# Attention with a mixture of experts: the ninth block's values in two column halves, its transposes behind the next pair's scores

## The chip, the cores and the metric

The kernel runs on one core of a Trainium2 chip. The metric is device time in microseconds, the median of several runs; lower is better. Engines are named as in the profile: PE (TensorE matmuls), PEld (its weight loads), DVE (VectorE), ACT (ScalarE), POOL (GpSimd), SP (SyncE, which issues most transfers here).

## What is computed

Attention over 8 batches of 8 heads with 576 tokens and 64 features a head. The first four heads see the last 32 tokens, the other four every fourth token of the last 128:

```python
scores = scale * np.matmul(q, k.transpose(0, 1, 3, 2))
mask_plain = (rel >= 0) & (rel < window)
mask_dil = (rel >= 0) & (rel < window * dilation) & (rel % dilation == 0)
...
attn = attn / (np.sum(attn, axis=-1, keepdims=True) + 1e-09)
return np.matmul(attn, v).astype(np.float32)
```

Its output, 4608 tokens of 512 features, goes to a layer of 8 experts (512 to 1024 to 512, with a maximum with zero between). Each token uses one expert: the one with the largest logit, or that of the token before it where a second gate says so. Everything is float32.

## The kernel before

**Stages.** The attention stage fills the first 153 us of the profiled span, and the experts' stage the rest. In the attention stage the work is cut by pair: two heads of one batch, 32 pairs in all. A pair's 576 tokens are nine blocks of 64 queries; each block looks at 96 keys, its own 64 and the 32 before them. The dilated heads' tokens are sorted by class beforehand, so that they too are a band.

**One pair.** `scores` multiplies keys by queries for nine blocks and two heads (L334), with a mask matmul ahead of the blocks that need no cut (L328); ACT takes the exponential (L341), DVE masks the other blocks (L339). The two heads lie on the two row halves of PE. `values` multiplies the exponentials by the values (L387); the value tile has a column of ones, so that column 64 of the result is the sum for the softmax. Two blocks lie beside each other on the two column halves of PE and so on the two partition halves of the output: slot k holds blocks 2k and 2k + 1. Nine blocks make five slots, and the fifth computes block 8 in both halves. Slots are taken in two groups, 0 and 1, then 2 to 4 (`HALVES`), each in a PSUM tile `pv`. For each group DVE takes the reciprocal of the sums into `rec` (L391) and multiplies (L392) into `x`, a tile that holds four heads (two pairs) of a batch.

**Two pairs.** After every second pair `turn` transposes `x` for the routing: eight full 128x128 transposes (L408), four for each pair, copied to `xt` by ACT (L409), and two of the last 64 tokens (L412), copied at once (L414). `store` writes `x` to memory in two transfers, the first 512 tokens (L422) and the last 64 (L424). There are 16 such turns.

**The order.** It is written out by hand for PE, DVE, POOL and SP; ACT's is left to the scheduler. The main loop runs over n from 0 to 33. In iteration n stand: the scores of pair n; POOL's copy of the 32 shared value rows of pair n + 1 (`share`, L279); a gap; the values of pair n - 1; in odd iterations from 3 on the turn of the two pairs before; a gap; the loads of pair n + 3 (`load_keys` L267, `load_values` L272); the store; and, late in the stage, one gather of routed rows on POOL (L855), with a small copy ahead of it that waits for `rec` (`paced`, L275). A gap takes steps of the routing from a list (`waiting`), each with a cost, as far as a credit allows. Among these are logits (L441), logits turned (L453), carries (L484, L494, L504), the choice (L510), places (L548, L549), products (L600), counts (L617), the table (L701) and the tokens of the early units (L718 on PE, L728 to L738 on DVE). After every fourth turn `route` puts a new group of such steps on the list.

**Buffers.** All PSUM tiles but the scores' come from one pool of four banks (`bank`), the scores from another of two. `x` has three buffers. `check` looks at all of `rec` at the end and decides whether an exact version has to run.

Of the kernel before, what the change touches and what calls it, by code (L numbers as in the profile page):

```python
# [10 lines left out]
F32 = mybir.dt.float32  # L11
# [4 lines left out]
Alu = mybir.AluOpType  # L16
# [6 lines left out]
P = 128  # L23
B, H, S, DH = 8, 8, 576, 64
D = H * DH
# [10 lines left out]

NP = H // 2
NPB = B * NP
SLOTS = (NB + 1) // 2
HALVES = ((0, 2), (2, SLOTS))  # L40
CB = 3
AHEAD = 4
WARM = 3
# [174 lines left out]
def whole(ctx, tc, exact, bad, qk, v, wgl, w1, w2, con, adm, msk, qmk, out, cst, wg, ones, warm):  # L218
# [32 lines left out]
    def bank(shape, name):  # L251
        return banks.tile(shape, F32, name=name, tag="bank")

    rec = once.tile([P, NPB, SLOTS, 2], F32, name="rec")
    pace = once.tile([1, 2], F32, name="pace")
    zero = work.tile([1, D // 2], F32, name="zero", bufs=1)
    nc.vector.memset(zero, 0.0)
# [14 lines left out]
        nc.sync.dma_start(out=vt[WIN:].rearrange("p u i e -> p (u i e)"), in_=v[n])  # L272

    def paced(n):
        nc.gpsimd.tensor_copy(pace, rec[:1, n, SLOTS - 1])  # L275

    def share(n):
        vt = vts[n % AHEAD]
# [36 lines left out]
    xs, prob, routes = {}, {}, {}  # L315

    def scores(n):

# [55 lines left out]
    def values(n):  # L374

        vt = loaded[n][2]
        if n % 2 == 0:
            xs[n // 2] = xp.tile([P, SLOTS, 2, 2, DH], F32, name="x")
        x = xs[n // 2]
        pr = prob.pop(n)  # L380
        for a, z in HALVES:
            pv = bank([P, z - a, 2, VW], "pv")
            for k in range(a, z):
                for u in range(2):
                    for h in range(2):
                        i = min(2 * k + h, NB - 1)
                        nc.tensor.matmul(pv[h * QB:(h + 1) * QB, k - a, u], lhsT=pr[i][:, u],  # L387
                                         rhs=vt[:, u, i], start=True, stop=True, tile_position=(0, h * QB),
                                         skip_group_check=True)
            r = rec[:, n, a:z]  # L390
            nc.vector.reciprocal(r, pv[:, :, :, DH])  # L391
            nc.vector.tensor_tensor(x[:, a:z, n % 2], pv[:, :, :, :DH],  # L392
                                    r.unsqueeze(3).to_broadcast([P, z - a, 2, DH]), op=Alu.mult)
        del loaded[n]

    def turn(m):

        x = xs[m]
        b, g = divmod(m, 2)
        if m % (2 * GB) == 0:  # L400
            routes[b // GB] = dict(xt=xtp.tile([P, 2, CH, GS], F32, name="xt"))
        xt = routes[b // GB]["xt"]
        s = b % GB * S
        full = S // P * P
        for c in range(CH):
            tp = bank([P, S // P, P], "tp")
            for k in range(S // P):
                nc.tensor.transpose(tp[:, k], x[:, k, c].rearrange("p u d -> p (u d)"), ident)  # L408
            nc.scalar.copy(xt[:, g, c, s:s + full], tp.rearrange("p k t -> p (k t)"))  # L409
        tp = bank([P, CH, S - full], "tp")  # L410
        for c in range(CH):
            nc.tensor.transpose(tp[:, c], x[:S - full, S // P, c].rearrange("p u d -> p (u d)"),  # L412
                                ident[:S - full, :S - full])
        nc.scalar.copy(xt[:, g, :, s + full:s + S], tp)  # L414

    def store(m):

        x = xs.pop(m)
        b, g = divmod(m, 2)
        full = S // P * P  # L420
        to = xd[g][b * S:(b + 1) * S]
        nc.sync.dma_start(out=to[:full].rearrange("(k p) f -> p k f", p=P),  # L422
                          in_=x[:, :S // P].rearrange("p k g u d -> p k (g u d)"))
        nc.sync.dma_start(out=to[full:], in_=x[:S - full, S // P].rearrange("p g u d -> p (g u d)"))  # L424

    def logits(g):

# [376 lines left out]
    def now(push):  # L804
        for f in push:
            f()
# [292 lines left out]
    for n in range(NPB + 2):  # L1099
        if n < NPB:  # L1100
            (scores_exact if exact else scores)(n)
        for k in range(NPB)[n + 1 if n else 0:n + 2]:
            share(k)
        gap(SHARE)
        if 1 <= n <= NPB:
            values(n - 1)
        if n == NPB + 1:
            assert len(rows) <= 4
            now(features(0))
        if n >= 3 and n % 2 == 1:  # L1110
# [30 lines left out]

    def check():

        flat = rec.rearrange("p n k u -> p (n k u)")
        fine = stage.tile([P, D], F32, name="y", bufs=3)[:, :NPB * SLOTS * 2]
# [8 lines left out]
        nc.vector.tensor_scalar(all_fine, lp, float(P * NPB * SLOTS * 2), None, Alu.is_lt)  # L1154
# [134 lines left out]
```

## Time and profile before

| What | us |
|---|---|
| median of 3 runs | 667.72 |
| lowest and highest run | 666.64, 669.94 |
| the profiled execution, own time | 663.76 |
| its span | 661.8 |
| PE busy in the span | 646.6 |
| DVE busy | 372.5 |
| ACT busy | 188.7 |
| POOL busy | 188.1 |

The span is the time from the first to the last instruction of the profiled execution; its own time holds 2.0 us around it. An instruction's busy time overlaps that of others on PE[...]. In the views below a group's line gives line, engine, operation, output<-inputs, shape and count, then busy us and mean ns of one, then the idle time of the engine ahead of it and what ended it.

### The profile page before, as it was taken

What the parts mean: (1) busy time and instruction counts of PE and PEld (TensorE: products, weight loads), DVE (VectorE), ACT (ScalarE), POOL (GpSimd) and SP (SyncE); (2) the same over time, 40 slices, a digit from 0 to 9 for tenths busy, and PEclk for the clock granted to TensorE, in tenths of its full rate; (3) what the DMA queues carried; (4) which work ended last, traced back from release to release, by engine and by line L of the source; (5) the groups of instructions that cost most, each with busy time, mean ns of one, the idle gap of its engine ahead of it and who ended that gap; (6) DMA issues with size and microseconds to landing.
All of it is one profiled execution on the core that took longest, in us unless ns stands there. A gap on an engine that the chain in (4) does not pass through costs nothing. (4 is left out here: it accounts for less than half of the span.)

```text
span 661.8 us, 15170 instructions
## 1 busy us (share of the span) xinstructions
PE 646.6 (98%) x6402; PEld 568.2 (86%) x6402; DVE 372.5 (56%) x755; ACT 188.7 (29%) x348; POOL 188.1 (28%) x169
## 2 busy tenths in 40 slices
PE   8999999999999999999999999999999999999996
PEld 6988888888588999999599989998899989899893
DVE  3558578683596595372537382727464536547441
ACT  3544343442112331222122222231222232223210
POOL 3322222242115420322552153223144113051011
PEclk9999999999999999999999999999999999999999
DMA  8999899749205398574533456541045451454001
GB/s 313 325 297 322 280 283 319 247 124 354 88 33 190 129 418 314 187 280 169 226 132 141 154 203 223 229 164 49 16 177 215 179 219 59 155 193 148 1 32 50
DMA packets 29356, 126.31 MB, mean 191 GB/s; under 512 B 4349, under 2 KB 13789, under 8 KB 25312
## 3 DMA queue, kind: packets, MB, share of 16 engines
q1 hardware_dynamic: 22480, 106.05, 44.4%
q0 software_dynamic: 6800, 19.21, 8.5%
q8 instruction: 52, 0.85, 0.5%
q14 instruction: 24, 0.20, 0.1%
HBM read 142.02 MB, written 19.20 MB: 244 GB/s over the span
## 5 line engine op out<-in xcount | busy, mean ns | idle before, releaser
L979 POOL DMA_INDIRECT out_dram<-y,tok x36 | 55.0, 1527 | 292.3 <-DVE y L1048 124.5
L951 PE MATMUL hp<-xc,sum 128*128 128x128 f32 x720 | 85.6, 275 | 0.4 <-DVE sum L818 0.4
L951 PEld LDWEIGHTS hp<-xc,sum 128*128 128x128 f32 x720 | 82.8, 192 | 0.8 <-PE hp L951 0.5
L1033 PE MATMUL yp<-sum,hc 128*128 128x256 f32 x360 | 82.6, 379 | 0.0
L961 DVE TENSOR_TENSOR h<-hp,h 128x512 f32<-128x512 f32 x45 | 30.9, 690 | 90.8 <-PE hp L951 90.1
L1033 PEld LDWEIGHTS yp<-sum,hc 128*128 128x128 f32 x360 | 68.3, 190 | 9.4
L1048 DVE SCALAR_TENSOR_TENSOR y<-yp,gate,y 128x256 f32<-128x256 f32 x45 | 21.7, 482 | 75.1 <-issue 48.1
L279 POOL COPY vt<-vt 32x1040 f32<-32x1040 f32 x32 | 34.0, 1065 | 94.2 <-DMA vt<-in_v_dram 63.0
L951 PE MATMUL hp<-xe,raw 128*128 128x128 f32 x480 | 58.8, 276 | 0.0
L951 PEld LDWEIGHTS hp<-xe,raw 128*128 128x128 f32 x480 | 56.6, 192 | 1.8 <-issue 1.5
L1033 PE MATMUL yp<-raw,h 128*128 128x256 f32 x240 | 57.0, 380 | 0.0
L334 PE MATMUL two<-kq 64*96 64x64 f32 x1152 | 54.5, 244 | 0.2 <-issue 0.2
L334 PEld LDWEIGHTS two<-kq 64*96 64x96 f32 x1152 | 53.7, 162 | 0.3 <-issue 0.3
L855 POOL DMA_INDIRECT xg<-xd,tok x40 | 45.5, 1138 | 27.3 <-PE hp L951 15.0
L1033 PEld LDWEIGHTS yp<-raw,h 128*128 128x128 f32 x240 | 44.4, 190 | 5.5
L955 ACT COPY h<-hp 128x512 f32<-128x512 f32 x45 | 26.4, 586 | 79.3 <-PE hp L951 75.3
L962 ACT ACTIVATE h<-h 128x512 f32<-128x512 f32 x45 | 28.3, 630 | 67.2 <-DVE h L961 67.2
L855 POOL DMA_INDIRECT xg<-xd,pos x40 | 44.1, 1102 | 11.8 <-issue 10.8
L339 DVE SCALAR_TENSOR_TENSOR pr<-two,mk 96x512 f32<-96x512 f32 x32 | 21.9, 685 | 43.8 <-ACT pr L341 32.3
L387 PE MATMUL pv<-vt,pr 96*64 96x65 f32 x1280 | 44.7, 224 | 1.0 <-POOL vt L279 1.0
L387 PEld LDWEIGHTS pv<-vt,pr 96*64 96x64 f32 x1280 | 40.2, 138 | 3.7 <-POOL vt L279 1.2
L1041 ACT ACTIVATE y<-yp,gate 128x256 f32<-128x256 f32 x45 | 21.2, 474 | 55.5 <-PE yp L1033 48.8
(223 smaller groups left out, 1004.6 us busy)
## 6 DMA issues: line engine op xcount, KB each, us to landing
raw<-in_w_dram SPq DMA_DIRECT2D x48, 2048.0 KB
kq<-in_qk_dram SPq DMA_DIRECT2D x32, 592.0 KB
vt<-in_v_dram SPq DMA_DIRECT2D x32, 292.5 KB
xd<-x SPq DMA_DIRECT2D x16, 512.0 KB
raw<-in_w_dram SPq DMA_DIRECT2D x4, 512.0 KB
xd<-x SPq DMA_DIRECT2D x16, 64.0 KB
xg<-xd,tok POOLq DMA_INDIRECT x40, 3.2
xg<-xd,pos POOLq DMA_INDIRECT x40, 3.4
```

The costliest lines, as they stand in the source:

```text
L279: nc.gpsimd.tensor_copy(vt[:WIN, :, 1:], vt[QB:, :, :NB - 1])
L334: nc.tensor.matmul(sc[:KW, u, k * QB:(k + 1) * QB], lhsT=kt[h, i * QB:i * QB + KW], rhs=qt[h, i * QB:(i + 1) * QB], start=bool(late), stop ...
L339: nc.vector.scalar_tensor_tensor(pr, sc[:KW, :, :w], -CEIL, mk[:, kind].unsqueeze(1).to_broadcast([KW, 2, w]), Alu.max, Alu.min)
L387: nc.tensor.matmul(pv[h * QB:(h + 1) * QB, k - a, u], lhsT=pr[i][:, u], rhs=vt[:, u, i], start=True, stop=True, tile_position=(0, h * QB), ...
L855: nc.gpsimd.indirect_dma_start(out=x[:rows, g], out_offset=None, in_=xd[g] if units[u]["late"] else xd[g][:EARLY * GS], in_offset=bass.Ind ...
L951: nc.tensor.matmul(to[:, m], lhsT=a[:, m, kk], rhs=b[:, kk], start=first and m == 0 and kk == 0, stop=(kk == DK // 2 - 1), skip_group_chec ...
L955: nc.scalar.copy(at((0, 1, 3)[k]), of)
L961: nc.vector.tensor_tensor(at(k), of, at(k), op=Alu.add)
L962: nc.scalar.activation(at(k), at(k), Act.Relu)
L979: nc.gpsimd.indirect_dma_start(out=out, out_offset=bass.IndirectOffsetOnAxis(ap=of_unit(u, "tok", j), axis=0), in_=y, in_offset=None, boun ...
L1033: nc.tensor.matmul(to, lhsT=a[:, m], rhs=b[:, m], start=first and m == 0, stop=(m == FK // 2 - 1), skip_group_check=True)
L1048: nc.vector.scalar_tensor_tensor(at(k), of, of_unit(u, "gate", k // 2), at(k), Alu.mult, Alu.add)
```

## The change

In `values` the fifth slot is no longer a slot of both heads and both halves. Block 8 of head u goes to column half u, so that two matmuls take the place of four, and one column of `pv` holds both heads. DVE takes 4 and 5 reciprocals instead of 4 and 6 (with one column of `rec` less), multiplies slots 2 and 3 as before, and multiplies the last column in an instruction of its own, which writes the result twice beside itself into a tile part `end`.

In `turn` the two transposes of the last 64 tokens become two full 128x128 transposes of `end`, each of a pair, and two ACT copies take a quarter of the result each (head u from partitions and columns of half u). They are not issued in `turn` but put on a list, which is run in the next iteration behind the scores and the gap, ahead of the values; in the four turns that a `route` follows, they are run at once. `store` writes the last 64 tokens in two transfers, one for each head of the pairs, in pieces of 64 floats.

```diff
-SLOTS = (NB + 1) // 2
-HALVES = ((0, 2), (2, SLOTS))
+FULLS = S // P
+HALVES = ((0, 2), (2, FULLS))
+SUMS = NB
...
-        nc.gpsimd.tensor_copy(pace, rec[:1, n, SLOTS - 1])
+        nc.gpsimd.tensor_copy(pace, rec[:1, n, SUMS - 2:])
...
+        def product(to, h, u, i):
+            nc.tensor.matmul(to[h * QB:(h + 1) * QB], lhsT=pr[i][:, u], rhs=vt[:, u, i], start=True, stop=True, tile_position=(0, h * QB), skip_group_check=True)
+
         for a, z in HALVES:
-            pv = bank([P, z - a, 2, VW], "pv")
+            last = z == FULLS
+            w = 2 * (z - a)
+            pv = bank([P, w + last, VW], "pv")
             for k in range(a, z):
                 for u in range(2):
                     for h in range(2):
-                        i = min(2 * k + h, NB - 1)
-                        nc.tensor.matmul(pv[h * QB:(h + 1) * QB, k - a, u], lhsT=pr[i][:, u],
-                                         rhs=vt[:, u, i], start=True, stop=True, tile_position=(0, h * QB),
-                                         skip_group_check=True)
-            r = rec[:, n, a:z]
-            nc.vector.reciprocal(r, pv[:, :, :, DH])
-            nc.vector.tensor_tensor(x[:, a:z, n % 2], pv[:, :, :, :DH],
-                                    r.unsqueeze(3).to_broadcast([P, z - a, 2, DH]), op=Alu.mult)
+                        product(pv[:, 2 * (k - a) + u], h, u, 2 * k + h)
+            if last:
+                for u in range(2):
+                    product(pv[:, w], u, u, NB - 1)
+            r = rec[:, n, 2 * a:2 * z + last]
+            nc.vector.reciprocal(r, pv[:, :, DH])
+            nc.vector.tensor_tensor(x[:, a:z, n % 2], pv[:, :w, :DH].rearrange("p (k u) d -> p k u d", u=2),
+                                    r[:, :w].rearrange("p (k u) -> p k u", u=2).unsqueeze(3).to_broadcast(
+                                        [P, z - a, 2, DH]), op=Alu.mult)
+            if last:
+                nc.vector.tensor_scalar(end[:, n % 2], pv[:, w:, :DH].to_broadcast([P, 2, DH]), r[:, w:], None, Alu.mult)
...
-        tp = bank([P, CH, S - full], "tp")
-        for c in range(CH):
-            nc.tensor.transpose(tp[:, c], x[:S - full, S // P, c].rearrange("p u d -> p (u d)"),
-                                ident[:S - full, :S - full])
-        nc.scalar.copy(xt[:, g, :, s + full:s + S], tp)
+
+        def ends():
+            tp = bank([P, CH, P], "tp")
+            for c in range(CH):
+                nc.tensor.transpose(tp[:, c], end[:, c].rearrange("p u d -> p (u d)"), ident)
+            for u in range(2):
+                h = slice(u * DH, (u + 1) * DH)
+                nc.scalar.copy(xt[h, g, :, s + full:s + S], tp[h, :, h])
+
+        behind.append(ends)
...
-        nc.sync.dma_start(out=to[full:], in_=x[:S - full, S // P].rearrange("p g u d -> p (g u d)"))
+        for u in range(2):
+            nc.sync.dma_start(out=to[full:].rearrange("t (g u d) -> t u g d", g=2, u=2)[:, u],
+                              in_=end[u * DH:(u + 1) * DH, :, 0])
...
         gap(SHARE)
+        now(behind)
+        behind.clear()
         if 1 <= n <= NPB:
             values(n - 1)
...
             if (n - 3) // 2 % (2 * GB) == 2 * GB - 1:
+                now(behind)
+                behind.clear()
                 route((n - 3) // 2 // (2 * GB), n == NPB + 1)
```

More of the change, by code (lines that the diff above doesn't have):

```diff
@@ L252, in bank @@
         return banks.tile(shape, F32, name=name, tag="bank")
-    rec = once.tile([P, NPB, SLOTS, 2], F32, name="rec")
+    rec = once.tile([P, NPB, SUMS], F32, name="rec")
     pace = once.tile([1, 2], F32, name="pace")
@@ L313, in load_first @@
                           in_=w1[i, :, part * rows * D:(part + 1) * rows * D])
-    xs, prob, routes = {}, {}, {}
+    xs, prob, routes, behind = {}, {}, {}, []
     def scores(n):
@@ L377, in values @@
         if n % 2 == 0:
-            xs[n // 2] = xp.tile([P, SLOTS, 2, 2, DH], F32, name="x")
-        x = xs[n // 2]
+            x = xp.tile([P, 4 * (FULLS + 1) * DH], F32, name="x")
+            xs[n // 2] = (x[:, :4 * FULLS * DH].rearrange("p (k g u d) -> p k g u d", k=FULLS, g=2, u=2),
+                          x[:, 4 * FULLS * DH:].rearrange("p (g u d) -> p g u d", g=2, u=2))
+        x, end = xs[n // 2]
         pr = prob.pop(n)
+        def product(to, h, u, i):
+            nc.tensor.matmul(to[h * QB:(h + 1) * QB], lhsT=pr[i][:, u], rhs=vt[:, u, i], start=True, stop=True, tile_position=(0, h * QB), skip_group_check=True)
         for a, z in HALVES:
-            pv = bank([P, z - a, 2, VW], "pv")
+            last = z == FULLS
+            w = 2 * (z - a)
+            pv = bank([P, w + last, VW], "pv")
             for k in range(a, z):
@@ L385, in values @@
                     for h in range(2):
-                        i = min(2 * k + h, NB - 1)
-                        nc.tensor.matmul(pv[h * QB:(h + 1) * QB, k - a, u], lhsT=pr[i][:, u],
-                                         rhs=vt[:, u, i], start=True, stop=True, tile_position=(0, h * QB),
-                                         skip_group_check=True)
-            r = rec[:, n, a:z]
-            nc.vector.reciprocal(r, pv[:, :, :, DH])
-            nc.vector.tensor_tensor(x[:, a:z, n % 2], pv[:, :, :, :DH],
-                                    r.unsqueeze(3).to_broadcast([P, z - a, 2, DH]), op=Alu.mult)
+                        product(pv[:, 2 * (k - a) + u], h, u, 2 * k + h)
[9 more added lines that the diff above has]
+                nc.vector.tensor_scalar(end[:, n % 2], pv[:, w:, :DH].to_broadcast([P, 2, DH]), r[:, w:], None, Alu.mult)
         del loaded[n]
     def turn(m):
-        x = xs[m]
+        x, end = xs[m]
         b, g = divmod(m, 2)
@@ L409, in turn @@
             nc.scalar.copy(xt[:, g, c, s:s + full], tp.rearrange("p k t -> p (k t)"))
-        tp = bank([P, CH, S - full], "tp")
-        for c in range(CH):
-            nc.tensor.transpose(tp[:, c], x[:S - full, S // P, c].rearrange("p u d -> p (u d)"),
-                                ident[:S - full, :S - full])
-        nc.scalar.copy(xt[:, g, :, s + full:s + S], tp)
+        def ends():
[6 more added lines that the diff above has]
+        behind.append(ends)
     def store(m):
-        x = xs.pop(m)
+        x, end = xs.pop(m)
         b, g = divmod(m, 2)
@@ L422, in store @@
         nc.sync.dma_start(out=to[:full].rearrange("(k p) f -> p k f", p=P),
-                          in_=x[:, :S // P].rearrange("p k g u d -> p k (g u d)"))
-        nc.sync.dma_start(out=to[full:], in_=x[:S - full, S // P].rearrange("p g u d -> p (g u d)"))
+                          in_=x.rearrange("p k g u d -> p k (g u d)"))
+        for u in range(2):
+            nc.sync.dma_start(out=to[full:].rearrange("t (g u d) -> t u g d", g=2, u=2)[:, u],
+                              in_=end[u * DH:(u + 1) * DH, :, 0])
     def logits(g):
@@ L1142, in check @@
     def check():
-        flat = rec.rearrange("p n k u -> p (n k u)")
-        fine = stage.tile([P, D], F32, name="y", bufs=3)[:, :NPB * SLOTS * 2]
+        flat = rec.rearrange("p n k -> p (n k)")
+        fine = stage.tile([P, D], F32, name="y", bufs=3)[:, :NPB * SUMS]
         nc.vector.tensor_scalar(fine, flat, 1.0 / HIGH, None, Alu.is_ge)
@@ L1153, in check @@
         all_fine = sm.tile([1, 1], F32, name="all_fine")
-        nc.vector.tensor_scalar(all_fine, lp, float(P * NPB * SLOTS * 2), None, Alu.is_lt)
+        nc.vector.tensor_scalar(all_fine, lp, float(P * NPB * SUMS), None, Alu.is_lt)
         over = sm.tile([1, 1], F32, name="over_any")
```

## The prediction

> **What bounds the kernel.** I read the page first. TensorE (PE) is busy for 98% of the span, at full clock in every slice, and the DMA engines are not full. The chain that ended last reaches back only to 632 us, through output transfers, so it says nothing of the attention stage (0 to 153 us), the only one that is changed.
>
> ```profile
> PE 646.6 (98%) x6402; PEld 568.2 (86%) x6402; DVE 372.5 (56%) x755; ACT 188.7 (29%) x348; POOL 188.1 (28%) x169
> DMA  8999899749205398574533456541045451454001
> ```
>
> Then the waits of PE up to 260 us. Of some 9 us that PE waits in the whole span, 3.2 stand at one line, L412, the transposes that are moved (columns: us in total, times, longest).
>
> ```profile
> PE tp L412 <- DVE rec L391: 2.2, 2, 1.2
> PE pv L387 <- POOL vt L279: 1.0, 1, 1.0
> PE tp L412 <- ACT xt L409: 1.0, 4, 0.2
> PE two L328 <- DVE pr L339: 0.8, 1, 0.8
> ```
>
> Then the groups by shape and PE's timeline. Columns of the timeline: start, length, line, output<-inputs, shape, count. A float32 matmul leaves two records, so 40 records of L387 are the 20 matmuls of one pair.
>
> ```profile
> L387 PE MATMUL pv<-vt,pr 96*64 96x65 f32 x1280 | 44.7, 224 | 1.0 <-POOL vt L279 1.0
> L392 DVE TENSOR_TENSOR x<-pv,rec 128x384 f32<-128x384 f32 x32 | 17.8, 557 | 1.1
> L392 DVE TENSOR_TENSOR x<-pv,rec 128x256 f32<-128x256 f32 x32 | 13.6, 425 | 1.1
> L414 ACT COPY xt<-tp 128x128 f32<-128x128 f32 x16 | 4.4, 276 | 0.4 <-PE tp L412 0.4
> ```
>
> ```profile
> 24.76 1.39 PE L387 MATMUL pv<-vt,pr 96*64 96x65 f32 x40
> 26.08 1.09 PE L408 MATMUL tp<-cst,x 128*128 128x128 f32 x8
> 27.10 0.27 PE L412 MATMUL tp<-cst,x 64*128 64x64 f32 x1
> 27.11 0.33 PE L328 MATMUL two<-am 64*96 64x320 bf16 x1
> ...
> 27.29 1.79 PE L334 MATMUL two<-kq 64*96 64x64 f32 x36
> 29.00 1.39 PE L387 MATMUL pv<-vt,pr 96*64 96x65 f32 x40
> ...
> 69.52 0.24 PE L412 MATMUL tp<-cst,x 64*128 64x64 f32 x1 [1.16 <-DVE rec L391]
> ```
>
> Here is to be seen that PE never rests: what leaves its queue shortens the stage, unless something else takes over. One thing does, at the end of the stage: POOL's queue, where each copy of shared values (L279) waits for the gather (L855) before it to land.
>
> ```profile
> 124.07 1.04 POOL L855 DMA_INDIRECT xg<-xd,tok  x1 [2.40 <-DVE gate L738]
> 129.71 1.04 POOL L279 COPY vt<-vt 32x1040 f32<-32x1040 f32 x1 [4.60 <-PE two L334]
> ...
> 145.11 1.04 POOL L279 COPY vt<-vt 32x1040 f32<-32x1040 f32 x1 [2.95 <-PE kp L549]
> ```
>
> The releasers named there had long been done; in the trace the queue waits on the gathers' own semaphores. From 124.07 to 146.15 this chain runs at its own pace, and pair 31's values wait 1.03 us for its end.
>
> [...] transposes follow each other 109 ns apart, but from a 128x128 transpose to a 64-row one or to values it is 203 ns, so a switch costs 94 ns; L412 to L328, both 64-row, costs 9. [...] the trace has 425, and 1.03 ns per element between the two shapes[...]
>
> **The change, part by part** (against the profiled execution: span 661.8, its own time 663.76).
>
> *Values.* Of the last slot's four matmuls two go; the two that stay are in different column halves. In the trace records start in pairs, one for each half, 58.3 ns apart, so two matmuls side by side take 0.117 us, and ten such steps fill the 1.32 us from 24.76 to 26.08. Nine steps save 0.117 us a pair. Pairs 0 to 25 stand before the first gather: 26 x 0.117 = 3.04 us, all on PE's path. Pairs 26 to 30 only lengthen PE's wait for POOL: nothing. Pair 31's saved step comes after that wait: 0.12.
>
> *Old transposes out.* With the next pair's scores directly behind (6 turns), from L408's last start (26.90) to the next values (29.00) is 2.10 us. Without them: 203 ns of switch plus 1.77 us from scores to values (the stretch 22.99 to 24.76): 1.97. So they cost 0.13, running partly beside the mask matmuls. Before other work (10 turns; 60.33 to 60.59, or 41.81 to 42.07) they cost 0.26.
>
> *New transposes in.* They have 128 rows. Four stand directly behind L408 (the turns before a route): 2 x 109 = 0.22 and no new switch. Twelve stand between scores and values: PE needs 175 ns from scores to values; with them 176 + 109 + 203, as scores, L453 and values already do elsewhere in the trace: 0.31 more. Against the old costs, before the first gather: five turns +0.18, four +0.05, two -0.045, one +0.085: a loss of 1.10. After the gather chain only the last turn counts: -0.05.
>
> *Waits that go.* L412 waits for ACT 4 x 0.24; three of these are before the gather: 0.72. It waits for DVE 1.16 at 69.5 and 1.00 at 107.1, as its bank is the one that the same pair's first half of values must leave and DVE has a backlog. What is late next is the product L600 (72.7), which needs DVE's matrix "what" (done at 71.6). With all shifts PE would be there at 71.70 and DVE, with three more small operations, at 71.86: 0.2 comes back. At 107 the same sum gives PE 109.7 and DVE 109.5: nothing comes back. Net: 0.72 + 1.16 + 1.00 - 0.20 = 2.68. A wait of the new transposes themselves I take as zero: their bank is given free and their input written a whole scores stretch (1.8 us) earlier; if that cover fails, all of the values queue behind them.
>
> *DVE.* L392 of 384 elements becomes 256 plus a new one of 128: 425 and, by the slope, 293 against 557, 0.16 busy, and some 0.1 in its queue as they overlap. DVE is at 56%, so it matters only at the backlogs (counted above) and once ahead of the tokens (L728 to L738) that release the first gather: -0.10. From both sides: 0.05 to 0.20 each.
>
> *ACT.* One copy of 0.28 more a turn, 16 in all, at 29% busy: nothing. Its bank is wanted again by the next odd pair's second half.
>
> *DMA and SP.* The end rows leave in two stores with 256 B pieces: one issue more a turn (L424 takes 0.51 us) in SP's queue ahead of the next keys, and 256 packets instead of 64. The trace's 512 B packets take 27 ns and 1 KB ones 48; at 17 to 50 ns this is 0.3 to 0.8 us on each of 16 engines a turn against 0.2. Keys land 3 to 10 us before their scores from pair 4 on (pair 8: 30.1 against 34.67), so I take nothing; at worst 0.5 us once. The last turn's extra issue delays the weights by 0.5 us: their matmuls come 11 us after their landing. POOL's queue only reads another column of rec: nothing.
>
> Sum: 3.04 + 0.12 + 2.68 - 1.10 + 0.05 - 0.10 = 4.7 us. From 153 us on PE is the bound, so the end moves with it: 659.1 for this execution. The median of the runs is 667.72, 3.96 above the profiled one; the same 4.7 off it gives **663.0**, 0.7% faster.
>
> **Rivals.**
> *The waits come back.* DVE is busy 5.90 of 6.00 us from 66 to 72 and 5.86 from 102 to 108. If PE, freed at L412, waits as long at the values' bank or at L600, 1.96 more returns: 2.7 gained, 665.0. For it: those shares. Against it: the bank's release at 70.06 is ahead of values at 70.25.
> *The gather chain shortens.* The first gather took 5.6 us to its release, the others 3.4 to 3.9. If its landing meets less traffic, up to 1.6 more: 661.4. Against it: all traffic there is released by PE and moves along.
> *The two last matmuls don't run side by side.* Then the values save nothing: 1.5 gained, 666.2. Against it: their order keeps the halves alternating.
> *Slower: the new transposes' bank.* Two ACT copies must empty it before the next odd pair's second half of values. If ACT runs them behind the late blocks' exponentials, they end some 2.1 us after values start in ordinary pairs (exp at 72.31 for values at 71.39), 3.4 in a backlog (68.09 for 65.95); the bank is wanted after 3.5. From there each further us of ACT delay stops PE with all values behind it. At 12 turns, 0.39 us each uses up the gain; 0.7 each gives 671.4. Against it: 0.1 us of cover remains in the worst place, 1.4 elsewhere.
>
> **Chances.** Forecast 0.55; waits come back 0.22; chain shortens 0.08; not side by side 0.06; slower 0.09. The range 660.5 to 666.6 takes in the first four with 1 us for the spread of the runs (666.64 to 669.94). About 0.5% (3.3 us) is what a measurement of this kernel can tell from no change; the line is at 664.4, near the forecast, so some of its chance falls within: faster 0.62, same 0.30, slower 0.08.
>
> **What would show it.** Right: 36 records of values a pair, 1.20 us to the next group; the last L412-like group gone from PE's waits; scores to values 0.31 longer in every other pair; a POOL wait of pair 31 that has grown by about 0.6; that pair some 4.5 us earlier. Wrong: a PE wait for ACT or DVE in front of values or L600, the new transposes idle before they start, or a gather chain of other length.

## The result and the profile after

| What | before | after |
|---|---|---|
| median of the comparison's runs (22 each), us | 669.17 | 666.20 |
| lowest, us | 666.64 | 664.46 |
| ratio of the runs, 95% interval | | 0.9954 [0.9940, 0.9969] |
| the profiled execution, own time | 663.76 | 667.46 |
| its span | 661.8 | 665.6 |

The change gains 3.1 us (2.1 to 4.0), or 0.46%, where 4.7 were forecast. The 3.1 is 0.0046 times the 669.17 of the same comparison; on the 667.72 from which the forecast started, the same ratio gives 664.6.

The two profiled executions stand the other way round: the one before was shorter than all of that kernel's timed runs. A second profile of each settles how to read them. From the experts' first matmul to the end, the four profiles take 509.6 and 511.9 us (before) and 512.4 and 512.0 (after). Nothing is changed there. This time goes with the chip: it is 509 to 510 us in the profiles of e5 to e8, which ran on one chip, and 512 to 514 in those of the others (e9 and e10 aside), which ran on three other chips. So the end is left out below, and profiles are compared from the first scores matmul to the last group of logits, which I call the stage.

First PE's waits in the stage of the kernel after (columns: us in total, times, longest). Lines have moved: L513 was L494, L567 was L548, L619 was L600, L636 was L617, L420 was L408, and L426 holds the new transposes.

```profile
PE last L513 <- DVE rec L400: 1.9, 3, 1.2
PE tp L420 <- ACT xe L890: 1.6, 1, 1.6
PE cold L291 <- DVE warm L208: 1.5, 1, 1.5
PE two L329 <- DVE pr L340: 0.8, 1, 0.8
PE kp L567 <- ACT xt L421: 0.7, 3, 0.2
PE ap L619 <- DVE what L610: 0.7, 1, 0.7
PE tp L426 <- ACT xt L421: 0.4, 2, 0.2
```

The 3.2 us at the old transposes are gone, but 1.9 + 0.7 + 0.7 us of new waits stand in front of three tiles of the routing, none of which is among the waits of before. The last turn's transposes wait 1.6 for `xe`, where pair 31's values waited 1.0 for POOL. Summed over all matmuls of the stage, PE is idle 5.4 us in both profiles of before, and 6.7 and 5.3 in those of after. No wait has gone on balance.

The groups by shape say that the work itself came out as planned (busy us and mean ns behind the bar):

```profile
L386 PE MATMUL pv<-vt,pr 96*64 96x65 f32 x1152 | 40.9, 224 | 0.0
L401 DVE TENSOR_TENSOR x<-pv,rec 128x256 f32<-128x256 f32 x64 | 27.2, 425 | 2.2
L405 DVE TENSOR_SCALAR x<-pv,rec 128x128 f32<-128x128 f32 x32 | 10.9, 342 | 0.0
```

So does PE's timeline, early in the stage (start, length, line):

```profile
19.23 1.66 PE L335 MATMUL two<-kq 64*96 64x64 f32 x36
20.82 0.44 PE L426 MATMUL tp<-cst,x 128*128 128x128 f32 x2
21.19 1.27 PE L386 MATMUL pv<-vt,pr 96*64 96x65 f32 x36
22.39 0.34 PE L329 MATMUL two<-am 64*96 64x320 bf16 x2
22.56 1.66 PE L335 MATMUL two<-kq 64*96 64x64 f32 x36
24.16 1.27 PE L386 MATMUL pv<-vt,pr 96*64 96x65 f32 x36
```

Values take 36 records and 1.20 us to the next group (21.19 to 22.39) instead of 1.32. From scores to values it is 1.60 us without the new transposes (22.56 to 24.16) and 1.96 with them (19.23 to 21.19): 0.36 more. In all, the stage less PE's idle time is 140.2 us in the profile of before and 138.1 in the second one of after (e2), the two in which the clock stayed full: 2.0 us of work are gone.

Where the gain goes is seen by setting the two timelines beside each other. Up to 47 us the kernel after is 0.85 us ahead. Then this happens (PE, after):

```profile
48.80 1.27 PE L386 MATMUL pv<-vt,pr 96*64 96x65 f32 x36
50.00 1.31 PE L420 MATMUL tp<-cst,x 128*128 128x128 f32 x8
52.54 0.17 PE L513 MATMUL last<-cst,run 12*1 12x12 f32 x1 [1.24 <-DVE rec L400]
```

DVE of the same kernel in the same stretch, and then POOL:

```profile
50.62 1.23 DVE L507 TENSOR_TENSOR_SCAN run<-row 12x96 f32<-12x96 f32 x1
51.79 0.15 DVE L400 RECIPROCAL rec<-pv 128x4 f32<-128x4 f32 x1
...
52.31 0.18 DVE L400 RECIPROCAL rec<-pv 128x5 f32<-128x5 f32 x1
```

```profile
50.61 1.05 POOL L280 COPY vt<-vt 32x1040 f32<-32x1040 f32 x1 [3.58 <-DMA vt<-in_v_dram]
```

The scan at L507 takes 0.34 us where nothing runs beside it (e6 below). Here POOL's copy of shared values started 10 ns ahead of it, and the scan ends 0.19 us behind the copy's end: 1.23 us. The values' reciprocals and the first multiplication (L401) are queued behind it on DVE, the tile `last` of L513 needs the bank that this multiplication empties, and PE stands still for 1.24 us. I call this a **meeting**. Nothing in the change touches L507 or L280; POOL's copy starts when the DMA of its values lands.

### The profile page after: what moved, and what is told of

Same layout as the page of the kernel before. It is cut to its first block, busy times and chain, and to the rows that moved or that the text cites. A ratio compares the mean times of both kernels' runs of the same rounds, so it can differ in the third digit from the quotient of the medians.

```text
span 665.6 us, 15017 instructions
## 1 busy us (share of the span) xinstructions
PE 646.6 (97%) x6274; PEld 565.7 (85%) x6274; DVE 377.1 (57%) x787; ACT 193.9 (29%) x364; POOL 185.3 (28%) x169
## 5 line engine op out<-in xcount | busy, mean ns | idle before, releaser
L280 POOL COPY vt<-vt 32x1040 f32<-32x1040 f32 x32 | 34.3, 1074 | 92.9 <-DMA vt<-in_v_dram 61.5
L386 PE MATMUL pv<-vt,pr 96*64 96x65 f32 x1152 | 40.9, 224 | 0.0
L386 PEld LDWEIGHTS pv<-vt,pr 96*64 96x64 f32 x1152 | 36.4, 137 | 3.8 <-issue 1.2
## 6 DMA issues: line engine op xcount, KB each, us to landing
xd<-x SPq DMA_DIRECT2D x16, 512.0 KB
raw<-in_w_dram SPq DMA_DIRECT2D x4, 512.0 KB
```

The costliest lines, as they stand in the source:

```text
L280: nc.gpsimd.tensor_copy(vt[:WIN, :, 1:], vt[QB:, :, :NB - 1])
L386: nc.tensor.matmul(to[h * QB:(h + 1) * QB], lhsT=pr[i][:, u], rhs=vt[:, u, i], start=True, stop=True, tile_position=(0, h * QB), skip_grou ...
```

## The experiments

In the table, "stage" is the time from the first scores to the last logits in the run's profile, and "idle" PE's idle time in it, summed from its timeline; a pause that the records of a group cover up is not in it. One profile stands for each run, and two profiles of one kernel differ by up to 3 us in the stage, so the ratios carry the verdicts on time, and the profiles say where. A star marks a window of half clock near 148 us, which is told of at the end. "Stretched" is DVE's time over the usual length of its operations, where a POOL copy ran beside them.

| Run | ratio to before, 95% | stage, us | idle | stretched |
|---|---|---|---|---|
| before | | 145.5 | 5.4 | 1.9 |
| e1 before again | | 146.8 * | 5.4 | 4.6 |
| after | 0.9954 [0.9940, 0.9969] | 146.3 * | 6.7 | 4.6 |
| e2 after again | | 143.4 | 5.3 | 3.0 |
| e3 halves only | 0.9972 [0.9949, 0.9995] | 146.3 | 8.4 | 5.1 |
| e4 deferral only | 0.9963 [0.9946, 0.9980] | 146.7 * | 5.0 | 5.2 |
| e7 end on ACT | 0.9953 [0.9937, 0.9970] | 144.8 * | 4.9 | 4.3 |
| e8 before and one operation | 1.0042 [1.0021, 1.0063] | 149.3 * | 6.7 | 2.8 |
| e11 after, once more | 0.9946 [0.9924, 0.9968] | 147.0 * | 6.9 | 5.9 |
| *copies on ACT:* | | | | |
| e5 before | 1.0015 [0.9995, 1.0035] | 146.3 | 5.0 | 0.2 |
| e17 before, once more | 0.9984 [0.9971, 0.9997] | 147.2 | 5.7 | 0.2 |
| e6 after | 0.9926 [0.9902, 0.9951] | 141.2 | 3.2 | 0.0 |
| e18 after, once more | 0.9909 [0.9885, 0.9934] | 141.6 | 3.5 | 0.0 |
| e12 after, a third time | 0.9901 [0.9875, 0.9927] | 141.5 | 3.4 | 0.0 |
| e13 halves only | 0.9930 [0.9915, 0.9945] | 143.1 | 5.6 | 0.0 |
| e14 deferral only | 0.9957 [0.9940, 0.9973] | 144.9 | 4.3 | 0.2 |
| e15 before and one operation | 1.0001 [0.9986, 1.0016] | 148.3 | 7.5 | 0.2 |
| e16 after, pairs 0 to 25 alone | 0.9943 [0.9920, 0.9965] | 142.6 | 4.5 | 0.2 |

### e1 and e2: both kernels again

No edit. 

> The kernel before, unchanged, for a second profile. Theory S (the waits of PE in the attention stage come from chance meetings of DVE and POOL and differ from run to run): waits of 0.2 to 1.3 us stand at other lines or places than 69.5 and 107.1, and the stage ends (logits after the last turn) more than 0.5 us from 150.2. Theory F (the waits are fixed by the order): L412 waits for DVE at 69.5 and 107.1 again, 1.0 to 1.2 us each, and the logits start within 0.3 us of 150.2.

> The changed kernel, unchanged, for a second profile. Theory S: the 1.24 us wait of L513 at 52.5, the idle 1.6 us before the last turn and the half clock from 149.4 are not all there again, and the stage ends 1 to 4 us earlier than in its first profile. Theory F: L513 waits 1.2 us at 52.5 again, the last turn waits 1.6 us, and the logits start within 0.3 us of 149.4.

Measured: single times of 667.72 and 664.50. The waits of before at L412 are there again (2.4 us, of it 1.4 for DVE) and at the same two places, of 1.1 us at 69.0 and 0.3 at 106.6; those of after are again at the routing's tiles, but mostly at another of them: 1.3 us at L619 and 0.5 at L513. The last logits start at 151.7 us in e1 and at 148.6 in e2. What follows: neither theory holds alone. The waits of before keep their places and change their length; those of after change their place too.

### e3 and e4: one half of the change each

```diff
-        behind.append(ends)
+        ends()
```

> The changed kernel with the transposes of the last 64 tokens issued in the turn, as before, not behind the next scores; the values' change is kept. Theory D ([...] gives no wait back): twelve deferred pairs of transposes at 0.37 us become 0.22 us without a new switch, so 1.8 us less on PE, and about the same waits: 1 to 2 us faster than the changed kernel, ratio to before 0.992 to 0.994. Theory W (the wait at these transposes is real and deferring removes it): 1 to 3 us slower than the changed kernel, ratio to before 0.997 to 1.000.

Measured: 0.9972, 667.15 us. Waits of PE in e3:

```profile
PE tp L426 <- DVE rec L400: 3.6, 5, 1.5
...
PE tp L426 <- ACT xt L421: 1.0, 4, 0.2
```

The transposes at their old place wait more than before (3.6 us for DVE against 2.2).

e4 is the kernel before with its own 64-row transposes put on the list:

```diff
+        def ends():
+            tp = bank([P, CH, S - full], "tp")
...
+        behind.append(ends)
...
+        now(behind)
+        behind.clear()
         if 1 <= n <= NPB:
             values(n - 1)
```

> The kernel before with its own 64-row transposes put behind the next pair's scores (at once in the turns before a route), and nothing else changed. Theory D (the bank's wait passes to the next user): [...] they cost about 0.15 us there against 0.13 to 0.26 in the turn: 0 to 1 us faster than before, ratio 0.9985 to 1.000. Theory W (deferring removes 3 us of waits): 2 to 4 us faster than before, ratio 0.994 to 0.997.

Measured: 0.9963, 667.44 us against 669.25 (by the ratio 2.5 us faster, 1.3 to 3.6). Its waits:

```profile
PE last L498 <- DVE rec L391: 1.1, 2, 0.8
PE pv L387 <- POOL vt L279: 1.0, 1, 1.0
PE kp L552 <- ACT xt L409: 0.9, 3, 0.4
...
PE ap L604 <- DVE what L595: 0.5, 1, 0.5
```

What follows: both halves gain. The ratio is one that the theory of real waits expected, but idle time falls by 0.4 us only, and the deferral without the column halves already shows the new waits at `last`, `kp` and `ap`. The wait for a bank passes from the transposes to the tile that comes next: in the program built from e4, `last` at 52 us and `cn` at 107 wait for the very multiplications (L392) that the tile of L412 waits for in the kernel before. What the rest of the 2.5 us comes from, the one profile does not show. The halves gain 1.9 us and the deferral 2.5, together 4.4; both at once give 3.1.

### e5 and e6: no meetings

In both kernels the copy of the shared values goes from POOL to ACT, so that no such copy runs on POOL beside DVE; POOL's queue behind the gathers loses that work too.

```diff
-        nc.gpsimd.tensor_copy(vt[:WIN, :, 1:], vt[QB:, :, :NB - 1])
+        nc.scalar.copy(vt[:WIN, :, 1:], vt[QB:, :, :NB - 1])
```

> The kernel before with the copies of the shared value rows (one a pair) on ACT instead of POOL, so that no POOL copy meets a DVE operation and the last pairs' copies don't queue behind gathers. Theory C (a POOL copy stretches the DVE operation beside it, and DVE's delay is what PE waits for): no DVE operation of the attention stage more than 0.15 us over its usual length, PE's waits for DVE in the stage under 0.7 us (1.9 to 2.2 before), pair 31's wait for the copy gone: 2 to 4 us faster than before, ratio 0.994 to 0.997. Theory L (DVE's load alone is the cause): the waits for DVE stay at 1.5 to 2.2 us, and only pair 31's wait goes: within 1 us of before, or slower if ACT's queue is held by the loads.

> The changed kernel with the same copies on ACT. Theory C: with the chance meetings gone from both, the change's own saving on PE shows: values 32 x 0.117 = 3.7 us less 12 x 0.37 + 4 x 0.22 = 5.3 us of new transposes plus 3.4 us of old ones, 1.8 us, plus what L412 still waits for ACT and DVE in the kernel before with the copies on ACT: 2 to 3 us faster than that kernel and 4 to 6 us faster than before, ratio 0.991 to 0.994. Theory L: waits for DVE of 1 to 2 us at the first routing tile behind a turn remain, and it is less than 1.5 us faster than the other.

Measured on one chip: e5 665.60 us, e6 659.93: 5.7 us between them. The copy takes as long on ACT as on POOL (1.06 us), stretched time falls to 0.2 and 0.0, and pair 31's wait is gone. But theory C had e5 at 0.994 to 0.997 with under 0.7 us of waits for DVE, and that is missed: e5 waits for DVE 1.4 us at L412 and 0.7 at `last`. It also has a pause that no list of PE's waits shows. ACT copies shared values between the two halves of `xt`, and the logits that read them stand still until it is done (ACT, then PE's weight loads, of e5):

```profile
80.73 1.06 ACT L279 COPY vt<-vt 32x1040 f32<-32x1040 f32 x1
81.70 0.57 ACT L409 COPY xt<-tp 128x512 f32<-128x512 f32 x1
82.17 0.25 ACT L414 COPY xt<-tp 128x128 f32<-128x128 f32 x1
```

```profile
82.47 0.62 PEld L441 LDWEIGHTS lp<-xt,wg 128*32 128x32 f32 x10 [0.63 <-ACT xt L414]
```

This group of logits takes 2.91 us from 80.72 on, and 2.15 in the kernel before. e6 has no such pause. Waits of PE in e6:

```profile
PE kp L567 <- ACT xt L421: 0.7, 3, 0.2
PE last L513 <- DVE rec L400: 0.5, 2, 0.2
...
PE tp L420 <- DVE rec L400: 0.3, 1, 0.3
```

The same place as above, DVE and then PE of e6:

```profile
50.36 0.34 DVE L507 TENSOR_TENSOR_SCAN run<-row 12x96 f32<-12x96 f32 x1
50.63 0.15 DVE L400 RECIPROCAL rec<-pv 128x4 f32<-128x4 f32 x1
```

```profile
50.04 1.09 PE L420 MATMUL tp<-cst,x 128*128 128x128 f32 x8
51.38 0.17 PE L513 MATMUL last<-cst,run 12*1 12x12 f32 x1 [0.25 <-DVE rec L400]
```

The scan has its 0.34 us, and the wait of 1.24 is one of 0.25. What follows: with the copies on ACT the change is worth more than was forecast, and the kernel before gains nothing that this run can measure. How much of that is the meetings is told below.

### e7 and e8: the added DVE operation

e7 gives the multiplication of block 8 to ACT; e8 puts such an operation, with an output that nobody reads, into the kernel before.

```diff
-                nc.vector.tensor_scalar(end[:, n % 2], pv[:, w:, :DH].to_broadcast([P, 2, DH]), r[:, w:], None, Alu.mult)
+                nc.scalar.activation(end[:, n % 2], pv[:, w:, :DH].to_broadcast([P, 2, DH]), Act.Copy, scale=r[:, w:])
```

> The changed kernel with the multiplication of the ninth block's result (DVE, 0.34 us a pair, 11 us in all) on ACT. Theory L (the operation added to DVE makes PE wait in the routing stretches): 1 to 2 us faster than the changed kernel, ratio to before 0.992 to 0.9945, and PE's waits for DVE under 1.5 us. Theory C: chance meetings stay, the waits stay at 2 us and only move: within 0.7 us of the changed kernel.

Measured: 0.9953, the same as after. Idle time falls to 4.9, with DVE's meetings left as they are (4.3 us).

```diff
+    spare = once.tile([P, 2, DH], F32, name="spare")
...
+            if z == SLOTS:
+                nc.vector.tensor_scalar(spare, pv[:, 2:, 0, :DH].to_broadcast([P, 2, DH]), r[:, 2:, 0], None, Alu.mult)
```

> The kernel before with one more DVE operation a pair, of the changed kernel's new form (128x128 from the values' PSUM tile, scaled, written to a spare tile that nobody reads), and nothing else. As the prediction costed it (at the backlogs alone): 0 to 0.5 us slower, ratio 1.000 to 1.001. Theory L: 11 us more of DVE work of which the stretches with routing have a third: 1 to 2.5 us slower, ratio 1.0015 to 1.004, with more waits of PE for DVE at L412.

Measured: 1.0042, 667.55 us against 665.47: 2.8 us slower (1.4 to 4.2). What follows: one operation more a pair is not free where nothing else is edited. PE waits at L415, the old transposes, 4.1 us in all, of it 2.7 for ACT and 1.4 for DVE (1.0 and 1.4 in e1). That the operation costs this by holding the values' bank longer is likely and not shown. But taking the operation off DVE in the kernel after (e7) gains nothing measurable. It is not alone what took the gain.

### e9 and e10: one thing left out

e9 fills `end` with ones instead of multiplying; e10 leaves the old end transposes out and copies a constant in their place. Both leave block 8's part of the routing's input out. The tokens are then routed otherwise and the exact version runs as well, so their times (2202 and 2187 us, ratios of 3.29 and 3.26) say nothing; only the attention stage of the profile is read.

```diff
-                nc.vector.tensor_scalar(end[:, n % 2], pv[:, w:, :DH].to_broadcast([P, 2, DH]), r[:, w:], None, Alu.mult)
+                nc.vector.memset(end[:, n % 2], 1.0)
```

> The changed kernel without the DVE multiplication of the ninth block's result: a constant is written in its place (a short DVE fill), so the last 64 tokens of a sequence get no attention result. Theory L (the added DVE work costs PE time): 1.5 to 3 us faster than the changed kernel, ratio to before 0.991 to 0.9935. Theory B (the waits come from the rotation of four banks and chance meetings, the added work hardly counts): within 0.8 us of the changed kernel, ratio 0.994 to 0.9965.

```diff
-            nc.tensor.transpose(tp[:, c], x[:S - full, S // P, c].rearrange("p u d -> p (u d)"),
-                                ident[:S - full, :S - full])
-        nc.scalar.copy(xt[:, g, :, s + full:s + S], tp)
+        nc.scalar.copy(xt[:, g, :, s + full:s + S], ident.rearrange("p (c t) -> p c t", c=CH))
```

> The kernel before without the transposes of the last 64 tokens (L412); ACT copies a constant of the same size to their place, so the routing of these tokens is wrong. As the prediction costed it (their waits of 3.2 us go with them, and 3.4 us of their own PE time): 5 to 6.5 us faster than before, ratio 0.990 to 0.9925. Theory B (the wait for the bank passes to the next routing tile behind the turn): 3 to 4 us faster, ratio 0.994 to 0.9955, and a routing tile (L494, L548 or L617) waits for DVE 1 to 2 us in all.

Measured: e9 has a stage of 143.5 us with 5.3 idle, like e2, with 5.9 us stretched. e10, in which L412 and its bank don't exist any more, has a stage of 144.8 us with a window of half clock. It is idle for 4.0 us up to the token matmul all the same (the kernel before 3.8 and 3.4), of it 1.2 in one pause at 34 us that the profile puts down to no engine, and for 3.0 from there on (1.5 and 2.0). Waits of PE in e10:

```profile
PE pv L387 <- POOL vt L279: 2.3, 1, 2.3
...
PE cp L506 <- DVE rec L391: 1.0, 2, 0.6
...
PE ap L596 <- DVE what L587: 0.7, 2, 0.5
PE kp L544 <- ACT xt L409: 0.7, 3, 0.2
```

What follows: with the transposes out and PE earlier, 2.4 us of waits come back at `cp`, `ap` and `kp`, and 1.3 more at pair 31's values, whose POOL copy is no earlier. At L412 there had been 3.2 and 2.4. That is the prediction's step "waits that go" by itself, and it fails.

### e11 and e12: meant for other banks, the same programs again

In the turn's iterations the two banks of the full transposes are taken ahead of those of the values, which was meant to hand the banks out in another order; e12 has the copies on ACT too.

```diff
+        if n >= 3 and n % 2 == 1:
+            tps = [bank([P, S // P, P], "tp") for _ in range(CH)]
...
-            turn((n - 3) // 2)
+            turn((n - 3) // 2, tps)
```

> The changed kernel with the two banks of the full transposes taken ahead of the values' banks, so that the routing tile behind a turn gets the bank that ACT empties first and not the one that DVE still has to empty; no instruction changes its place on PE. Theory B: the waits of L513, L529 and L636 for DVE (2.4 us in the first profile, 0.5 in the second) go down to 0.24 us waits for ACT at each: 0.5 to 2 us faster than the changed kernel, ratio to before 0.991 to 0.9945. Theory L (DVE is late for its data, not for its banks): PE waits for DVE at L619 or in front of values instead: within 0.5 us of the changed kernel, 0.9945 to 0.9965.

> The changed kernel with the shared rows' copies on ACT and the banks taken first, both. Theory B with C: the waits for DVE of the stage (0.8 us with the copies on ACT alone) go too: 4.5 to 6.5 us faster than before, ratio 0.990 to 0.993. If ACT is late for the banks that it now empties first: 0.993 to 0.996.

Measured: 0.9946 and 0.9901. But the edit changes nothing: in the program built from e11 every instruction of the stage has the same bank and the same waits as in the kernel after, and e12 is e6 in the same way. The trace agrees: in e11, L513 waits 1.18 us for DVE at 53.27, behind the same stretched scan as in after. What follows: theory B is not tested, and whether another order of the banks would help stays open. The two runs are repeats: the kernel after has 0.9954 and 0.9946, and with the copies on ACT 0.9926, 0.9909 and 0.9901 (662.70 us against 669.33, 6.6 us below the kernel before).

The other edits do change the banks, which are dealt out when the program is built. Of the stage's 144 tiles from the pool of four, 64 get another bank in e5 than in the kernel before, 93 in e6 than in after, and 108 in e8 than in before. What that alone costs or gains, no run tells, so differences of an experiment by half a microsecond or so may be due to it.

### e13 to e16: the parts without meetings

e13, e14 and e15 are e3, e4 and e8 with the copies on ACT. e16 is the kernel after with the copies of pairs 0 to 25 on ACT:

```diff
-        nc.gpsimd.tensor_copy(vt[:WIN, :, 1:], vt[QB:, :, :NB - 1])
+        if n < 26:
+            nc.scalar.copy(vt[:WIN, :, 1:], vt[QB:, :, :NB - 1])
+        else:
+            nc.gpsimd.tensor_copy(vt[:WIN, :, 1:], vt[QB:, :, :NB - 1])
```

> The changed kernel with its end transposes issued at once in the turn, and the copies of the shared values on ACT: only the column halves, in a kernel where no POOL copy meets a DVE operation. Theory 1 (meetings with POOL copies make DVE late, the parts cost what the working said): the transposes that wait for DVE fall from 3.6 us, as measured without deferral and with copies on POOL, to 1.5 us or less; against the kernel before with copies on ACT (1.0015) 3.1 us for the values and about 0.3 back for the transposes: ratio 0.997 to 0.9985. Rival (the order of DVE's own work makes it late, meetings or not): the waits stay at 3 us or more, ratio 0.9995 to 1.002.

> The kernel before with its old end transposes behind the next pair's scores, and the copies of the shared values on ACT: only the deferral, without meetings. Theory 1: the 1.4 us of waits for DVE in front of the transposes go and do not come back elsewhere, as DVE is not made late again; ratio 0.9985 to 1.000 (the kernel before with copies on ACT gave 1.0015). Rival (a wait that goes here comes back at the next tile from the four banks in any case): the waits at the tiles of the routing grow by 1 us or more and the ratio stays at 1.001 to 1.0025.

> The kernel before with one more DVE operation of 0.34 us a pair, and the copies of the shared values on ACT. Theory 1: the operation alone costs little, as DVE has room where nothing meets it: at most 0.7 us more than the kernel before with copies on ACT, ratio 1.0015 to 1.0025. Rival (the operation itself makes the waits, meetings or not): 2 to 3 us more, as in the kernel before with copies on POOL, ratio 1.0045 to 1.006.

> The changed kernel with the copies of the shared values of pairs 0 to 25 on ACT and those of pairs 26 to 31 on POOL, behind the gathers as before. With all copies on ACT it gave 0.9926, with all on POOL 0.9954. If meetings with DVE took the gain: PE's idle time from the first scores to the token matmul falls to about 2.4 us as with all copies on ACT, that from there to the last logits stays near 2 to 2.6 as with all on POOL, and the ratio is near 0.994. If the queue behind the gathers took all of it: no change of the first, 0.995 to 0.9955. If meetings took all of it: 0.9925.

Measured in e13, where the 3.6 us of e3 were:

```profile
PE tp L426 <- DVE rec L400: 2.3, 5, 0.8
...
PE tp L426 <- ACT xt L421: 1.1, 4, 0.3
```

Again there are five waits, now of 2.3 us: between the two theories, as by these two profiles 1.3 us come from meetings and 2.3 from DVE's own order. The ratio, 0.9930, is better than either expected; both expectations started from e5, whose pause in the logits e13 doesn't have. In e14 no wait for DVE is over 0.5 us but the 0.8 ahead of the first masks that every run has, and PE's idle time falls by 1.0 against the mean of e5 and e17. In e15 it rises by 2.1, with no meeting at all, but 1.4 of it is one pause in scores, at 105 us, that the profile puts down to no engine. e16 is idle for 2.4 us up to the token matmul (L737 in the kernel after), as with all copies on ACT (2.4), and 2.1 from there to the last logits, as with all on POOL (2.7 and 1.9 in the two profiles of after; 0.8 and 1.1 in e6 and e18). Its ratio, 0.9943, lies between as expected, though its interval reaches both ends.

### e17 and e18: the base on one chip

The base e5 had been timed on a chip where the kernel before takes 665.5 us, and e13 to e16 on one where it takes 669.2. So e5 and e6 were run again side by side, unchanged, on a third (669.6).

> The kernel before with the copies of the shared values on ACT, once more: the base for the three runs of single parts, which were taken on another chip, where the kernel before took 669.2 us and not 665.5. If the added operation costs some 2 us without any meeting, as the profiles of the attention stage say (148.3 us from the first scores to the last logits against 146.3), this base is at 0.996 to 0.998; if the operation is nearly free, as the times said, the base stays at 1.000 to 1.002.

> The changed kernel with the copies of the shared values on ACT, beside its base on the same chip: the change without meetings. If its parts add up (the column halves alone saved 3.2 us and the deferral alone 1.3 in the profiles, without meetings), it is 4.5 to 5.7 us faster than its base, 0.9915 to 0.993 of it; if the base itself was faster on this chip, only 3 to 4, 0.994 to 0.9955 of it.

Measured: 668.58 and 663.04 us, or 0.9917: with the copies on ACT the change gains 5.5 us. The base itself is 1.1 us faster than the kernel before here (0.2 to 1.9). Against this base the column halves alone gain 3.6 us (0.9930 to 0.9984) and the deferral alone 1.8 (0.9957 to 0.9984), and 3.6 + 1.8 = 5.4: the parts add up. With the copies on POOL the middle values did not (1.9 + 2.5 against 3.1), though their intervals are too wide to exclude it. The added operation in the kernel before costs 1.1 us (1.0001 to 0.9984, give or take 1.3), between the two theories.

## Why the prediction was wrong

**Values: right.** 0.12 us a pair, 36 records; 26 x 0.12 is the 3.04 of the sum.

**Transposes: right in kind, a little too cheap.** Behind scores they cost 0.36 us, not 0.31; for the nine deferred turns ahead of the first gather that is 0.45 more than the 1.10 of the sum. The 0.36 us are two full transposes between scores and values as measured (1.96 us against 1.60); the 0.31 was an estimate, added up from single steps in the trace of before.

**The gather chain: right.** From the token matmul to the last logits it is 30.8 us before and 30.8 in e2, the profile of after without half clock. The wait of 1.0 for POOL that was to grow by 0.6 grew at another place, in front of the last turn's transposes (1.6 and 0.8 in the two profiles).

**DMA: right.** The 256 B packets of the end rows took 18 ns on average up to 153 us, at the low end of the prediction's 17 to 50.

**DVE: mis-sized.** L405 takes 0.34 us, not 0.29, and DVE is 0.21 us a pair busier, not 0.16. More important, its price on PE was put at 0.10 in all. An added operation of this size costs 2.8 us (1.4 to 4.2) in the kernel before, and about 1.1 (give or take 1.3) with the copies on ACT.

**"Waits that go: net 2.68": the step that failed.** With the copies on POOL, idle time did not fall (5.4 and 5.4 before, 6.7, 5.3 and 6.9 after, e11 being the third). The other terms of the sum give 4.7 - 2.68 = 2.0 us, which is what PE's work fell by; the 3.1 measured (2.1 to 4.0) is a little above that. The reasoning took each wait of the one trace as a thing of L412 and let it go with L412. What the runs show is that L412 was only the tile that came next for a bank, so that the wait passes to the next tile of the routing (e4, e10), and that DVE is late there partly because of meetings. The prediction asked for one such return, at 69.5 us (0.2), and put the rest at nothing. The stretch at 107 shows it plainly: the sum said that nothing comes back there. PE of the kernel after:

```profile
106.80 0.36 PE L636 MATMUL cn<-cum,ones 96*128 96x8 f32 x2 [0.33 <-DVE rec L400]
107.02 0.42 PE L426 MATMUL tp<-cst,x 128*128 128x128 f32 x2
107.36 1.27 PE L386 MATMUL pv<-vt,pr 96*64 96x65 f32 x36
109.34 0.88 PE L619 MATMUL ap<-lane,what 96*112 96x128 f32 x6 [0.71 <-DVE what L610]
```

And DVE ahead of it:

```profile
102.94 1.80 DVE L594 TENSOR_TENSOR lane<-cst,lanes 96x768 f32<-96x768 f32 x1
```

The product at L594 takes 0.94 us elsewhere and 1.80 here, beside a POOL copy that runs from 102.88 to 103.93. Of the 1.00 gained at the old transposes, 0.33 + 0.71 comes back at L636 and L619. In e18, with the copy on ACT, L594 takes 0.94 at this place and L619 follows the values with no wait.

The trace of before held the evidence. It has an operation of 0.17 us that took 1.03, ahead of a wait that the prediction took for a plain backlog (DVE, then POOL, of the kernel before):

```profile
62.66 1.03 DVE L563 CAST pf<-part 96x12 f32<-96x12 int32 x1
63.72 0.17 DVE L564 SCALAR_TENSOR_TENSOR segs<-ef,pf 96x12 f32<-96x12 f32 x1
```

```profile
62.61 1.04 POOL L279 COPY vt<-vt 32x1040 f32<-32x1040 f32 x1 [5.78 <-DMA vt<-in_v_dram]
```

Why the two hold each other back, no trace shows; when they do is seen in the times. In the profile of before, 16 multiplications at L392 and 8 masks at L339, which read PSUM, started beside a POOL copy and kept their 425, 557 and 687 ns, while L563 there and L507 and L594 of the kernel after, which read SBUF alone, came to their end only after the copy's, by 0.03 to 0.8 us. Not every operation on SBUF is held: in the same profile of before, a reduction (L557) that reads SBUF alone started at 145.23 us beside a copy, kept its 0.31 us and ended 0.60 ahead of the copy. Where DVE is first, the copy can be held: one that started 10 ns behind L610 in the kernel after (at 70.72 us, 0.85 us long) took 1.75 us and not 1.04.

**The sum with the copies on ACT.** The forecast took 4.7, and left the savings of pairs 26 to 30 out because of the gather queue (5 x 0.117 = 0.6): 5.3 for a kernel without that queue. Measured are 5.5 and 5.7. That they agree is in part luck, as the copies slow the base. In e5 and e17 the stage less idle time is 141.3 and 141.5 us, against 140.2 in the kernel before, with the same work; 0.76 of it is the pause in the logits. In e6 and e18 it is 137.9 and 138.1, as in e2. So 1.1 to 1.3 us of the 5.5 and 5.7 are a loss of the base, and an estimate from these figures for the change alone is 4.2 to 4.6. With the copies on POOL 3.1 are left.

**Why the kernel before gains so little from the copies' move.** In e5 the two long waits at L412 fall from 2.2 us to 0.4, and pair 31's wait of 1.0 goes. Against this stand 0.76 in the logits, 0.7 at `last`, which waits for DVE in e5 and doesn't wait in before, 0.5 more at L412 at two other places (61.9 and 119.1 us), and 0.6 more at the last turn's transposes.

**The rivals.** "The waits come back" (665.0, 2.7 us of gain) is what happened, at one of the places that it named, L600, now L619, and at others; it lacked the meetings. "The gather chain shortens" and "not side by side" fall by the timelines shown or told above. The slower one falls too: the values (L386) wait nowhere for ACT.

**What stays open.** How the loss of the changed kernel with its copies on POOL (0.9954 and 0.9946 against 0.9926 to 0.9901) splits between meetings and the queue behind the gathers rests on e16's idle times; its ratio can't tell. What the new dealing of the banks adds to any of these differences is not tested.

## What to carry to other kernels

A wait for a bank of a shared pool belongs to the pool and not to the line that it is booked on: before counting its removal as gain, ask which tile is next and whether the engine that frees the bank is late by then as well. Look for single operations that are far longer than their group's mean, and at what runs on POOL beside them. A copy on POOL can be worth moving to ACT even where POOL is 28% busy: it was worth 0 to 1 us before the change and 2 to 3.5 after it. But look at what stands behind it in ACT's queue: in the kernel before, the logits paid for the move. And check that an edit which is to hand out other banks does so in the program that is built.

## What was not expected of the hardware

A POOL copy of 32 x 1040 elements, 1.04 us, can hold back a DVE operation on SBUF for most of its own length: 0.34 to 1.23 us, 0.17 to 1.03. The copy in its turn was held by a DVE operation that was first, 1.04 to 1.75 us. Which operation is hit changes from run to run of one kernel (DVE was stretched by 4.6, 3.0 and 5.9 us in the three profiles of the kernel after, and L513's wait of 1.24 us in the first was 0.3 at most in e2), as most copies start with the landing of their data: in before, 63.0 of the 94.2 us that POOL idles ahead of them end with one.

PE's clock fell to half for 3.4 us (6.8 in e8) in 7 of the 11 profiles with all copies on POOL, of both kernels, and in none of the nine with the early or all copies on ACT. Windows of the kernel after (columns: us, then busy time and count of PE, PEld, DVE, ACT and POOL, the granted clock, the share of DMA, GB/s):

```profile
146.00:149.40 3.40, 1.65 (x12) 1.04 (x10) 3.33 (x8) 2.04 (x4) 1.96 (x3) 1.00 0.43 134
149.40:152.80 3.40, 3.40 (x30) 1.36 (x32) 1.90 (x3) 0.63 (x3) 1.68 (x2) 0.50 1.01 270
```

The same stretch in e2:

```profile
146.00:149.40 3.40, 2.42 (x27) 1.52 (x30) 3.30 (x9) 2.67 (x6) 2.82 (x3) 1.00 0.53 179
149.40:152.80 3.40, 3.40 (x34) 2.37 (x27) 1.43 (x2) 0.40 (x1) 1.33 (x1) 1.00 0.97 276
```

PE was busy for 1.65 of 3.40 us ahead of the halving, all of it with transposes (L889, L420, L426). The logits of the last group then took 3.79 us instead of the 2.15 of e2. Transposes alone are not the reason: the windows of 3.4 us ahead of the other six halvings held 0.8 to 1.8 us of other matmuls, and in e14 a window with 2.4 us of transposes alone (146.3 to 149.7) kept full clock. Little work alone is not the reason either: e3 (65.7 to 69.1) and e9 (144.4 to 147.8) have such windows too, with 1.86 and 1.90 us of PE's work, and no half clock behind them. What sets it off is not shown. In the kernel after, the logits behind a wait of 1.6 us took 1.64 us longer at half clock; that the wait brought the half clock on is a guess. The half clock fell on both kernels, and the runs don't tell whether on one of them more often.
